# Another way to turn float64 weights into float32, a planner's order, and additions moved to VectorE

## The chip, the cores and the metric

The kernel runs on one core of a Trainium2 chip. The metric is the device time of one launch in microseconds (us). Three runs of the kernel before gave 1403.98, 1405.87 and 1405.85 us; the median is 1405.85.

## The reference

Three blocks follow one another, for a batch of 4, 448 tokens and 768 channels:

```
attention:  scores = q k^T / 8;  30 * tanh(scores / 30);  softmax;  times v        (12 heads of 64)
mixer:      u = x + (relu(x^T w_tok1) w_tok2)^T;   x = u + relu(u w_ch1) w_ch2     (768 -> 1536 -> 768)
FNet:       u = x + real(fft(fft(x, tokens), channels));  un = (u - mean) / std(u)
            out = u + relu(un w_ch1) w_ch2                                         (768 -> 3072 -> 768)
```

All weights of the two mixer blocks come as float64 (the generator scales float32 by a float64 number), so the kernel gets 64-bit words and has to make float32 of them.

## The kernel before, in words

**Precision.** Each float32 operand of the large products is split into a high part in the fast format (fp32r) and a low part, the difference. A product is three matmuls: high with high (L248), high weight with low data (L249), low weight with high data (L250); the helper is `mm3`. Each is 448 columns wide.

**Stages.** Attention runs first, in 24 pairs of heads. Then comes the first pair of channel products (`c1`, `c2`): 6 groups of 2 x 128 hidden channels, the first 3 in `group`, the others as visits. Between them and the last pair the Fourier step runs (`fold`, `transform`), spread over the visits. The second pair (`m1`, `m2`) has 12 groups for one half of the batch, again as visits, and then 6 Strassen groups (`up_steps`, `down_steps`) for the other half and for the combined blocks. `fold_in`, `fold_out`, `last15`, `last67` and `last23` add up the result tiles `z` at the end, and `store` writes them.

**A visit** has six steps. In each step `down` makes one tile of the output in PSUM (12 matmuls) and adds it into `z`. Between the steps the weights of the next visit are asked for, and at steps 2 and 3 the upper product of the next visit runs (`up`, 36 matmuls each), followed by `hidden`, which makes the relu and the split. A weight tile holds both halves of the 128 x 768 weights, and there are four such slots (`w`): two lower weights of this visit, two upper ones of the next.

**Weights.** `piece` makes a weight tile from a float64 block: `convert`, then `halves` (a ScalarE copy for the high part, a subtraction for the low one on VectorE or GpSimd). `convert` loads the block so that a byte lands ahead of each word, and then works in two strands. ScalarE makes a power of two from the top byte in three `Relu` steps (clamped from below, from above, and turned round), VectorE shifts the low word and sets an exponent (L359), adds the two powers as 16-bit words, and multiplies mantissa and power (L368). `convert_v`, for the token weights and the first two `c1` blocks, does it with VectorE steps alone but one (L313 to L323). In the second pair most pieces are also written to DRAM (`put`, `keep`) and fetched again for the Strassen groups (`fetch`, `fetch_x`); `combine` makes the Strassen sums of four pieces with subtractions on VectorE or GpSimd. Sixteen pieces are made ahead (`ahead`), during the first three groups of the first pair.

**The order.** The program's order on every engine comes from `Plan.run`, which is run when the program is built. Every operation has costs by engine (`v(n)` for VectorE, `vp(n)` for VectorE or GpSimd, whichever ends first in the plan, `a(n)` for ScalarE), worked out from the width n and from a fixed part in `fixed`. The planner keeps the operations sorted by their place in the code plus a shift by key (`SHIFT`), looks at the first few hundred, and takes the one that can start first; of those within 0.1 us, the one that stands first. `fixed` holds 0.065, 0.05 and 0.16 us (VectorE, ScalarE, GpSimd) while attention is described, and is set to 0.15, 0.14 and 0.3 before the rest is. Two `c1` blocks and the first splits (`split_u`) belong to the rest but are placed among attention.

Of the kernel before, what the change touches and what calls it, by code (L numbers as in the profile page):

```python
# [34 lines left out]
G = 2  # L35
RCOL = 904
TW = 8 * NE
MIN_NORMAL = 1.125 * 2.0 ** -15
SK1, SK2 = 3, 2
# [16 lines left out]
class Op:  # L56
# [9 lines left out]
    "den": -2446, "den<": -1603, "den>": -713, "exp": -90, "gather": -60, "late": 0, "wx": -40, "piece": -40, "exp<": -590, "exp>": -922, "load": 61,  # L66
# [143 lines left out]
def kernel(  # L210
# [58 lines left out]
    def t(n):  # L269
        return {"T": n / 2210}  # L270
# [60 lines left out]
    def convert(src, rows, cols, x=None):  # L331
# [12 lines left out]
        def cat(i):  # L344
            return cv()[i][:rows, :cols]

        def power(out, src, scale, bias, reads, writes):
            copy(cols, out, src, reads, writes, AF.Relu, scale=scale, bias=float(bias))
# [16 lines left out]
        def value():  # L365
            return (x() if x else raw().rearrange("p a b -> p (a b)").bitcast(F32))[:rows, :cols]
# [25 lines left out]
    def piece(src, x=None, k=None, dve=False):  # L392
        w, ws = w_slot()
        if dve:
            convert_v(src, 128, DM, part(w, 0), part(w, 1), ws[1:], [w])
        else:
            value, key = convert(src, 128, DM, x)
            halves(DM, value, part(w, 0), part(w, 1), [key, w], ws[1:])
            if k is not None:
                put(value, [key], k)  # L400
        return w, ws
# [333 lines left out]
    def phase_ce():  # L735
# [18 lines left out]
        def cut(q, w, f, kc):  # L754
            ws, wr = w[kc // NJ if q else f]
            c = f * NS + kc % NJ * 128 if q else kc * 128
            return ws, wr, slice(c, c + 128)
# [15 lines left out]

        def hidden(ps, y=None, fine=False):
            rh, rl = r_slot(F32R), r_slot(F32R)
            for bs in ((0,), (1,)) if fine else ((0, 1),):
                b0, n = bs[0], len(bs)
                kp, kh, kl = ([(x, b) for b in bs] for x in (ps, rh, rl))

                def at(x, b0=b0, n=n):  # L780
                    return pair(x)[:, b0:b0 + n, :]

                def src(b0=b0, n=n):
                    return ps()[:, b0:b0 + n, :S]

                if y is None:
                    copy(n * S, lambda at=at: at(rh), src, kp + [ps, rh], kh, AF.Relu)
                    pl.op(v(n * S), lambda e, at=at, src=src: V.scalar_tensor_tensor(
                        out=at(rl), in0=src(), scalar=0.0, in1=at(rh), op0=ALU.max, op1=ALU.subtract
                    ), kp + kh + [ps, rh, rl], kl)  # L790
                else:
                    pl.op(v(n * S), lambda e, at=at, src=src: V.scalar_tensor_tensor(
                        out=src(), in0=src(), scalar=0.0, in1=at(y), op0=ALU.max, op1=ALU.mult
                    ), [y, ps], kp)
                    copy(n * S, lambda at=at: at(rh), src, kp + [ps, rh], kh)
                    tt(v(n * S), lambda at=at: at(rl), src, lambda at=at: at(rh), ALU.subtract,
                       kp + kh + [ps, rh, rl], kl)
            return rh, rl

        def down(q, ws, r, bp, kc, y=None, apart=False):  # L800
            ps = mm_slot()
            zz = z[bp][kc]


            def mm(b, ps=ps):
                for fs in [[f] for f in range(G)] if apart else [list(range(G))]:
                    reads = [ps]
                    for f in fs:
                        reads += cut(q, ws, f, kc)[1] + list(r[f, bp]) + [(x, b) for x in r[f, bp]]

                    def mms(e, fs=fs):
                        for f in fs:
                            rh, rl = r[f, bp]
                            w, _, s = cut(q, ws, f, kc)
                            mm3(ps()[:, b, :S], w()[0][:, s], w()[1][:, s],
                                pair(rh)[:, b, :], pair(rl)[:, b, :], f == 0, f == G - 1)

                    pl.op(t(3 * len(fs) * S), mms, reads, [(ps, b)])

            def add(b0, n, ps=ps):  # L820
                tt(v(n * S), lambda: zz[:, b0:b0 + n, :], lambda: ps()[:, b0:b0 + n, :S], lambda: zz[:, b0:b0 + n, :],
                   ALU.add, [ps] + [(ps, b) for b in range(b0, b0 + n)], zk(bp, kc)[b0:b0 + n])

            mm(0)
            mm(1)
            if y is not None:
                pl.op(v(W2), lambda e: V.tensor_tensor(out=both(ps), in0=both(ps), in1=pair(y), op=ALU.mult),
                      [y, ps], [(ps, b) for b in range(2)])
            add(0, 2)

# [330 lines left out]
        wu = [piece(c1[f], dve=True) for f in range(G)]  # L1161
        split_u(0)
        split_u(1)

# [5 lines left out]
        def group(w1, w2, g, wu, u, nxt, between):  # L1170
# [15 lines left out]
            for bp in range(NB2):  # L1186
                for i, kc in enumerate(KORD):
                    down(0, wd, r, bp, kc)
# [66 lines left out]
        UPS, UPS2 = (2, 3), (2, 3)  # L1255
# [20 lines left out]
        AHEAD = [(n % 2, n // 2, n < 4 * SK2) for n in range(16)]  # L1276
# [12 lines left out]
        seq = [(0, g, bp) for bp in range(NB2) for g in range(NB, NGC)]  # L1289
        seq += [(1, g, 0) for g in range(NGM)]  # L1290
        kept = {}

        sh = [[None] * (NGM // 2) for _ in range(2)]
        held = {}

        def combine(q, g):
            x11, x21, x12, x22 = xs = [held.pop((q, 4 * g + i), None) or u_slot(F32) for i in ((0, 1, 2, 3) if q else (0, 2, 1, 3))]
            for x, i in ((1, 2), (3, 3), (0, 0), (2, 1)) if not q else ((1, 1), (3, 3), (0, 0), (2, 2)):
                if xs[x].first is None:
                    get(lambda x=x: xs[x]()[:, :DM], [], [xs[x]], fh[q][4 * g + i])  # L1300
# [11 lines left out]
        JOBS = {(4, 2): (0, 0), (5, 2): (1, 0), (6, 2): (0, 1), (7, 2): (1, 1)}  # L1312

        def weights(q, g, f, n):
            if q:
                k = G * g + f
                if (n, k) in early:
                    return fetch(early[n, k])
# [532 lines left out]
```

## Time and profile before

| | |
|---|---|
| median of three runs | 1405.85 us |
| profiled execution | 1406.29 us, its span 1404.4 us |
| TensorE matmul busy | 1365.7 us, 97% |
| VectorE busy | 1073.5 us, 76% |
| ScalarE busy | 704.1 us, 50% |
| GpSimd busy | 321.5 us, 23% |
| mean granted TensorE clock | 0.994 |

The span runs from the first to the last instruction. PE is TensorE, DVE is VectorE, ACT is ScalarE, POOL is GpSimd, SP is SyncE, which issues the DMAs. Nearly all elementwise operations are recorded by helpers, so L279 is any operation of two tensors and L276 any ScalarE step; the tile names tell them apart (`z<-mm,z` adds a PSUM tile into the output, `r<-mm,r` is the low half of a hidden tile). Matmuls overlap, so their durations add up to more than the time that passes. A row of the windows view gives a stretch (from:to in us), its length, the busy time and the number of instructions of PE, PEld (its weight loads), DVE, ACT and POOL, then the granted TensorE clock as a share of full speed, the DMA engines' busy share and GB/s. In other rows an arrow `<-` behind a number names what ended the idle time or the wait.

### The profile page before, as it was taken

How to read it: one execution, taken by the hardware profiler on the slowest of the kernel's cores; microseconds unless marked ns; L12 is line 12 of the kernel's file. 1: busy time of each engine (PE TensorE's matmuls, PEld its weight loads, DVE VectorE, ACT ScalarE, POOL GpSimd, SP SyncE). 2: the span in 40 equal slices, each digit the busy share in tenths (PEclk: the TensorE clock that was granted, in tenths of full speed). 3: DMA queues.
4: the chain of work that ended last, by engine and by line, in shares of the span. 5: the costliest groups of instructions: out<-in, count | busy, mean ns of one | idle time of the engine just before them, and what ended most of it. 6: DMA issues, size and time to landing. Idle time of an engine off the chain costs nothing.

```text
span 1404.4 us, 18761 instructions
## 1 busy us (share of the span) xinstructions
PE 1365.7 (97%) x7470; PEld 1135.0 (81%) x7470; DVE 1073.5 (76%) x1153; ACT 704.1 (50%) x824; POOL 321.5 (23%) x169
## 2 busy tenths in 40 slices
PE   8899999999999999999998999999999999999996
PEld 3344444599999999899998989988989998999996
DVE  7999988566776756557889699888977646667688
ACT  7878887576555544123233235444544553543432
POOL 4342433100000001000001122432314404414354
PEclk9999999999999999999999999999999999999999
DMA  4223221015666566512231168787868433344452
GB/s 125 86 73 105 83 73 47 7 68 157 247 201 194 193 222 207 160 46 91 90 136 57 46 223 298 272 309 259 301 229 298 152 113 100 103 124 133 130 178 99
DMA packets 67353, 211.90 MB, mean 151 GB/s; under 512 B 7552, under 2 KB 8960, under 8 KB 67266
## 3 DMA queue, kind: packets, MB, share of 16 engines
q1 hardware_dynamic: 66112, 208.08, 44.4%
q0 software_dynamic: 1152, 2.62, 0.7%
q8 instruction: 59, 0.97, 0.3%
q14 instruction: 28, 0.23, 0.0%
q10 hardware_dynamic: 2, 0.00, 0.0%
HBM read 145.30 MB, written 65.37 MB: 150 GB/s over the span
## 4 chain that ended last, share of the span: by engine, by line
PE 70%; DVE 15%; ACT 6%; DMA 5%; issue 2%; POOL 1%; SPq 0%; DVEq 0%; ACTq 0%; POOLq 0%
PE mm L249 20%; PE mm L248 20%; PE mm L250 20%; DVE t L279 3%; PE av L579 3%; DVE m L279 2%; DMA raw<-in_m_dram 2%; DMA wl<-kept 2%; PE sc L511 2%; DVE z L279 2%; ACT t L536 2%; ACT t L516 2%; PE av L595 2%; DVE u L279 2%; PE mx L706 1%
## 5 line engine op out<-in xcount | busy, mean ns | idle before, releaser
L249 PE MATMUL mm<-u,wh 128*128 128x448 f32 x798 | 293.7, 368 | 0.2 <-DVE u L279 0.2
L248 PE MATMUL mm<-u,wh 128*128 128x448 f32 x774 | 284.9, 368 | 4.9 <-DVE z L279 3.3
L250 PE MATMUL mm<-u,wl 128*128 128x448 f32 x774 | 284.6, 368 | 2.3 <-DMA wl<-kept 2.3
L279 DVE TENSOR_TENSOR z<-mm,z 128x896 f32<-128x896 f32 (+1 forms) x210 | 214.0, 1031 | 62.8 <-PE mm L250 61.4
L248 PE MATMUL mm<-r,wh 128*128 128x448 f32 x696 | 255.7, 367 | 0.7 <-DVE r L279 0.3
L249 PE MATMUL mm<-r,wh 128*128 128x448 f32 x678 | 249.4, 368 | 6.9 <-DVE r L279 6.6
L250 PE MATMUL mm<-r,wl 128*128 128x448 f32 x696 | 254.9, 366 | 0.0
L249 PEld LDWEIGHTS mm<-u,wh 128*128 128x128 f32 x798 | 151.1, 189 | 13.0 <-DVE u L279 0.6
L248 PEld LDWEIGHTS mm<-u,wh 128*128 128x128 f32 x774 | 146.5, 189 | 18.1 <-issue 3.7
L250 PEld LDWEIGHTS mm<-u,wl 128*128 128x128 f32 x774 | 146.5, 189 | 15.3 <-DMA wl<-kept 2.7
L276 ACT ACTIVATE cva<-raw 128x768 bf16<-128x768 int8 x70 | 63.4, 906 | 172.0 <-DVE u L368 66.4
L249 PEld LDWEIGHTS mm<-r,wh 128*128 128x128 f32 x678 | 127.8, 188 | 19.7 <-DVE r L279 8.7
L248 PEld LDWEIGHTS mm<-r,wh 128*128 128x128 f32 x696 | 131.2, 188 | 13.0 <-ACT r L276 0.8
L250 PEld LDWEIGHTS mm<-r,wl 128*128 128x128 f32 x696 | 131.2, 188 | 10.9
L528 POOL PARTITION_ALL_REDUCE mb<-m x48 | 93.6, 1997 | 166.9 <-DVE m L279 151.0
L276 ACT ACTIVATE r<-mm 128x896 fp32r<-128x896 f32 (+5 forms) x81 | 66.6, 826 | 119.2 <-PE mm L250 54.6
L279 DVE TENSOR_TENSOR t<-t,mb 112x1792 f32<-112x1792 f32 x48 | 107.3, 2254 | 5.5 <-POOL mb L528 5.4
L516 ACT ACTIVATE t<-sc,scl 112x896 f32<-112x896 f32 x96 | 92.4, 1004 | 12.4 <-PE sc L511 6.4
L276 ACT ACTIVATE wh<-wl 128x768 fp32r<-128x768 f32 x57 | 48.1, 845 | 95.3 <-DMA wl<-kept 93.8
L511 PE MATMUL sc<-qr 64*112 64x448 f32 x384 | 88.1, 569 | 7.7 <-ACT t L516 7.7
L536 ACT ACTIVATE t<-t,cap_sb 112x1792 f32<-112x1792 f32 x48 | 85.3, 1789 | 14.4 <-DVE t L279 14.1
L579 PE MATMUL av<-t,v 112*32 112x448 f32 x768 | 78.2, 542 | 2.0 <-ACT t L536 1.6
(205 smaller groups left out, 2238.1 us busy)
## 6 DMA issues: line engine op xcount, KB each, us to landing
raw<-in_m_dram SPq DMA_DIRECT2D x48, 767.6 KB, 5.1
wl<-kept SPq DMA_DIRECT2D x86, 384.0 KB, 3.5
kept<-u SPq DMA_DIRECT2D x60, 384.0 KB, 5.3
raw<-in_c_dram SPq DMA_DIRECT2D x22, 767.6 KB, 5.1
kept<-y SPq DMA_DIRECT2D x32, 384.0 KB, 5.7
wh<-kept SPq DMA_DIRECT2D x29, 384.0 KB, 3.1
raw<-kept SPq DMA_DIRECT2D x29, 384.0 KB, 3.1
qr<-in_qk_dram SPq DMA_DIRECT2D x23, 448.0 KB, 3.3
```

The costliest lines, as they stand in the source:

```text
L248: T.matmul(out=dst, lhsT=wh, rhs=xh, start=first, stop=False, skip_group_check=more)
L249: T.matmul(out=dst, lhsT=wh, rhs=xl, start=False, stop=False, skip_group_check=more)
L250: T.matmul(out=dst, lhsT=wl, rhs=xh, start=False, stop=last, skip_group_check=more)
L276: pl.op(a(n), lambda e: A.activation(out=out(), in_=src(), func=func, **kw), reads, writes)
L279: pl.op(engs, lambda e: eng[e].tensor_tensor(out=out(), in0=in0(), in1=in1(), op=op), reads, writes)
L511: T.matmul(out=ps()[:CP, k, :S], lhsT=qr()[d, S + c * CP:S + (c + 1) * CP], rhs=qr()[d, :S], start=True, stop=True)
L516: pl.op(a(W2, 0.06), lambda e, c=c, ps=ps: A.activation(out=tl()[:, c], in_=ps()[:CP, :, :S], func=AF.Tanh, scale=scl[:CP, 0:1]), [ps, tl] ...
L528: pl.op({"P": 1.9}, lambda e, k=k: P.partition_all_reduce(mb()[:, k], mx()[:, k], CP, bass_isa.ReduceOp.max), [mx, mb], [kb], hold=0.75)
L536: pl.op(a(2 * W2, 0.1), lambda e, k=k: A.activation(out=tl()[:, :, k], in_=tl()[:, :, k], func=AF.Exp, scale=cap_sb[:CP, 0:1]), [tl], [ke])
L579: T.matmul(out=ps()[d, :S], lhsT=vv()[:, c, d], rhs=tl()[:, c, hd], start=(c == 0), stop=(c == NCH - 1))
L595: T.matmul(out=ps()[32 * k:32 * k + 32, :S], lhsT=ones[:CP, 0:32].bitcast(F32), rhs=tl()[:, c, hd], start=(c == 0), stop=(c == NCH - 1))
L706: T.matmul(out=ps()[:, :S], lhsT=channels_of(rt()[:, tb, c], kc % NJ), rhs=wt[:, tb, :], start=False, stop=last, skip_group_check=True)
```

## The change

`convert` gets other steps. The top byte goes through one `Relu` and two `Prelu` steps on ScalarE: the first clamps it from below, the second bends it at the other end (the negative side is scaled by 2^-40, the positive one kept), the third turns it into the exponent field of a float32 as an integer. VectorE then makes one `scalar_tensor_tensor`: the low word shifted right by 5, or'ed with that field. The shift L359 and the 16-bit addition go.

```diff
-        power(lambda: cat(0), top, 2048.0, (7 - 16 * 56) * 128, [raw], [cv, ca])
-        power(lambda: cat(1), top, -2048.0, 32768 - (7 + 16 * 72) * 128, [raw, cv], [cf])
-        power(lambda: cat(1), lambda: cat(1), -1.0, 32768, [cv], [cf])
-        pl.op({"V": 0.07 + cols / 1920}, lambda e: V.tensor_scalar(
-            out=word(), in0=word(), scalar1=5, scalar2=112 << 23,
-            op0=ALU.logical_shift_right, op1=ALU.bitwise_or,
-        ), [], [raw])
-        tt({"V": 0.07 + cols / 1920}, lambda: cat(0).bitcast(U16), lambda: cat(0), lambda: cat(1), ALU.add,
-           [cv, cf], [ca])
...
+        copy(cols, step, top, [raw], [cv, ca], AF.Relu, bias=72.0)
+        copy(cols, step, step, [cv], [ca], AF.Prelu, scale=-1.0, bias=16.0, alpha=KINK)
+        copy(cols, field, step, [cv, ca], [cf], AF.Prelu, scale=-FIELD / KINK, bias=-112.0 * FIELD, alpha=KINK)
         pl.op(v(cols), lambda e: V.scalar_tensor_tensor(
-            out=value(), in0=word().bitcast(F32), scalar=-256.0, in1=cat(0), op0=ALU.mult, op1=ALU.mult,
-        ), [raw, cv, ca], [x or raw])
+            out=value(I32), in0=word(), scalar=5, in1=field(), op0=ALU.logical_shift_right, op1=ALU.bitwise_or,
+        ), [raw, cv, cf], [x or raw])
```

The step lengths of the planner change later than before: `fixed.update` moves behind the two `c1` blocks and the first splits. The additions of the Strassen groups into `z` (`gather`) lose their shift of -60 places; the additions of the visits get the same key, with a shift of 0.

```diff
-    "den": ..., "gather": -60, "late": 0, ...
+    "den": ..., "gather": 0, "hid": 0, "late": 0, ...
...
         wu = [piece(c1[f], engs=v) for f in range(G)]
         split_u(0)
         split_u(1)
+        fixed.update(V=0.15, A=0.14, P=0.3)
...
-        fixed.update(V=0.15, A=0.14, P=0.3)
         phase_ce()
```

All additions of `z` tiles to one another at the end may only run on VectorE, and the last tile is added in two halves:

```diff
-            tt(vp(S), lambda: a[:, 1, :], lambda: a[:, 1, :], lambda: a[:, 0, :], ALU.add, ka[:1], ka[1:])
+            tt(v(S), lambda: a[:, 1, :], lambda: a[:, 1, :], lambda: a[:, 0, :], ALU.add, ka[:1], ka[1:])
             for x, k in ((zl, kc), (zh, NJ + kc)):
-                tt(vp(W2), lambda x=x: x, lambda x=x: x, lambda: a, ALU.add, ka, zk(1, k))
+                tt(v(W2), lambda x=x: x, lambda x=x: x, lambda: a, ALU.add, ka, zk(1, k))
... (the same in fold_out, last15 and last67)
         def last23(kc, ps):
-            gather(1, kc, 0, 2, ps, 0, False)
-            store(1, kc, kc == NJ - 1)
+            end = kc == NJ - 1
+            for b in range(2) if end else (0,):
+                gather(1, kc, b, 1 if end else 2, ps, b, False)
+            store(1, kc, end)
```

The visits are rewritten as two classes, `First` and `Half`, with the same matmuls. One order changes: the second lower weight of a visit of the second pair is asked for ahead of step 1, behind the upper weights of the next visit; before, it was asked for after step 0, ahead of them. The pieces made ahead come in another order (`AHEAD`: four of `m1`, four of `m2`, and so on, instead of one of each in turn), and as many of them as before.

```diff
-                if q and i == 0 and len(x[4]) < 2:
-                    x[4].append(weights(q, g, 1, 1))
-                if i == (0 if q else 1) and not ending:
-                    a_, b_, c_ = seq[n + 1]
-                    nxt = visit(a_, b_, c_, [weights(a_, b_, f, 0) for f in range(G)])
...
+                if i == 1:
+                    x.below(1)
+                x.down(i, kc)
...
+                if i == int(one):
+                    nxt.above()
+                if i in UPS:
+                    if i == UPS[0]:
+                        nxt.below(0)
+                    nxt.up(UPS.index(i))
```

## Rows read from the trace of the kernel before

**Rows 1.** Windows by stage; the columns stand in the section on the profile above.
```profile
0.00:290.00 290.00, 276.01 (x2001) 134.17 (x2002) 246.00 (x235) 219.68 (x236) 94.28 (x54) 1.00 0.24 72
290.00:830.00 540.00, 532.48 (x2760) 491.52 (x2760) 392.21 (x489) 221.76 (x275) 35.24 (x23) 0.99 0.44 146
830.00:1060.00 230.00, 225.47 (x1093) 205.85 (x1092) 201.66 (x217) 117.86 (x145) 63.45 (x33) 0.99 0.78 276
1060.00:1355.00 295.00, 293.26 (x1439) 269.71 (x1439) 192.99 (x179) 131.08 (x153) 104.42 (x49) 1.00 0.46 146
1355.00:1404.40 49.40, 38.44 (x184) 33.71 (x182) 40.68 (x37) 13.72 (x19) 24.11 (x10) 0.97 0.32 112
sum 1404.40, PE 1365.66 PEld 1134.96 DVE 1073.54 ACT 704.10 POOL 321.49; mean PE 273.13 PEld 226.99 DVE 214.71 ACT 140.82 POOL 64.30
```

**Rows 2.** Waits of TensorE, whole run: us in total, times, longest.
```profile
PE sc L511 <- ACT t L516: 7.7, 16, 1.7
PE mm L249 <- DVE r L279: 6.6, 6, 1.8
PE mm L248 <- DVE z L279: 6.4, 3, 3.3
PE mm L250 <- DMA wl<-kept: 2.3, 1, 2.3
```

**Rows 3.** The same windows view, right after a long wait.
```profile
767.40:773.00 5.60, 5.56 (x15) 4.98 (x16) 5.60 (x6) 1.66 (x2) 0.00 (x0) 0.51 0.00 0
```

**Rows 4.** Groups by form, whole run: name, count, busy us, mean ns, idle before.
```profile
L276 ACT ACTIVATE cva<-raw 128x768 bf16<-128x768 int8 x70 | 63.4, 906 | 172.0 <-DVE u L368 66.4 <-DMA raw<-in_m_dram 33.8 <-DMA raw<-in_c_dram 32.3
```

**Rows 5.** Groups by form on VectorE, 830 to 1060 us.
```profile
L368 DVE SCALAR_TENSOR_TENSOR u<-raw,cva 128x768 f32<-128x768 f32 x31 | 34.3, 1105 | 1.2
L279 DVE TENSOR_TENSOR cva<-cva,cvf 128x768 uint16<-128x768 bf16 x31 | 22.0, 710 | 7.4 <-ACT cvf L276 7.2
L359 DVE TENSOR_SCALAR raw<-raw 128x768 int32<-128x768 int32 x31 | 21.7, 701 | 2.5 <-DMA raw<-in_m_dram 2.5
```

**Rows 6.** Timeline of VectorE, 150 to 166 us: start, us, engine, line, operation.
```profile
159.52 0.98 DVE L317 SCALAR_TENSOR_TENSOR cva<-raw,cva 128x768 int32<-128x768 int32 x1
160.54 1.57 DVE L320 SCALAR_TENSOR_TENSOR cva<-raw,cva 128x768 int32<-128x768 int32 x1
```

**Rows 7.** Waits of TensorE, 830 to 1060 us.
```profile
PE mm L249 <- DVE r L279: 4.3, 4, 1.8
```

**Rows 8.** Timeline before the wait that ends at 1037.82 us.
```profile
1033.33 1.97 DVE L279 TENSOR_TENSOR wl<-u,wh 128x768 fp32r<-128x768 f32 x1 [1.78 <-ACT wh L276]
...
1035.22 0.54 DVE L279 TENSOR_TENSOR cva<-cva,cvf 128x768 uint16<-128x768 bf16 x1
...
1037.82 0.47 PE L249 MATMUL mm<-r,wh 128*128 128x448 f32 x1 [1.84 <-DVE r L279]
```

**Rows 9.** Group of ScalarE's table loads, whole run.
```profile
L1710 ACT ACT_TABLE_LOAD x1 | 1.3, 1283 | 1.3 <-PEq L1836 1.3
```

**Rows 10.** Groups by form behind 1355 us.
```profile
L279 POOL TENSOR_TENSOR z<-z 128x896 f32<-128x896 f32 x6 | 15.8, 2642 | 4.8 <-DVE z L279 4.8
L279 DVE TENSOR_TENSOR z<-z 128x896 f32<-128x896 f32 x6 | 10.2, 1722 | 0.0
...
L279 DVE TENSOR_TENSOR z<-mm,z 128x896 f32<-128x896 f32 x3 | 3.2, 1084 | 0.7 <-PE mm L250 0.7
```

**Rows 11.** Timeline of the end (seven stores are merged in one row).
```profile
1383.95 0.47 PE L249 MATMUL mm<-r,wh 128*128 128x448 f32 x1 [1.64 <-DVE r L279]
...
1394.45 6.20 SPq L1167 DMA_DIRECT2D out_dram<-z  x7
...
1395.48 0.47 PE L248 MATMUL mm<-y,wh 128*128 128x448 f32 x1 [2.89 <-DVE z L279]
...
1398.22 1.62 DVE L279 TENSOR_TENSOR z<-mm,z 128x896 f32<-128x896 f32 x2 [0.74 <-PE mm L250]
```

**Rows 12.** Windows view of the stretch before the last freed tile.
```profile
1376.10:1394.30 18.20, 14.84 (x72) 12.95 (x70) 18.10 (x14) 3.32 (x5) 12.32 (x5) 1.00 0.00 1
```

More of the change, by code (lines that the diff above doesn't have):

```diff
@@ L342, in top, with step, field, value @@
             return raw().bitcast(I8)[:rows, :cols, 4]
[L344 to L348, printed above, removed]
+        def step():
+            return cv()[0][:rows, :cols]
+        def field():
+            return cv()[1].bitcast(I32)[:rows, :cols]
+        def value(dt=F32):
+            return (x().bitcast(dt) if x else raw().rearrange("p a b -> p (a b)").bitcast(dt))[:rows, :cols]
         pl.op(
@@ L771, in up, with hidden @@
             return ps
-        def hidden(ps, y=None, fine=False):
+        def hidden(ps, y=None):
+            pl.key = "hid"
             rh, rl = r_slot(F32R), r_slot(F32R)
[L776 to L797, printed above, removed]
@@ L1275, in phase_ce @@
         HL = 8
-        AHEAD = [(n % 2, n // 2, n < 4 * SK2) for n in range(16)]
+        AHEAD = [(q, 4 * g + i, not g) for g in range(2) for q, i in
+                 ((0, 0), (0, 1), (0, 2), (0, 3), (1, 0), (1, 2), (1, 1), (1, 3))]
         def between_c(g):
@@ L1288, in phase_ce @@
         ys = [None, None]
[L1289 to L1290 removed]
         kept = {}
[L1293 removed]
+        NG = NGM // 2
+        sh = [[None] * NG for _ in range(2)]
         held = {}
         def combine(q, g):
[L1297 to L1300, printed above, removed]
+            ix = (0, 1, 2, 3) if q else (0, 2, 1, 3)
+            x11, x21, x12, x22 = xs = [held.pop((q, 4 * g + i), None) or u_slot(F32) for i in ix]
+            for n in (1, 3, 0, 2):
+                if xs[n].first is None:
+                    get(lambda n=n: xs[n]()[:, :DM], [], [xs[n]], fh[q][4 * g + ix[n]])
             sh[q][g] = ks = [home() for _ in range(4)]
@@ L1341, in weights, with __init__, above, below @@
             return w, ws
-        def ups(x, f):
-            q, g, bp, w, wd, r = x
-            if not q or f == 0:
-                wd.append(weights(q, g, f, 1))
-            r[f, bp] = hidden(up(q, w, f, bp, (u, un)[q]), ys[bp] if q and g else None)
-        def visit(q, g, bp, w):
-            return [q, g, bp, w, [], {}]
+        class First:
+            def __init__(self, g, bp):
+                self.g, self.bp, self.wd, self.r, self.order = g, bp, [], {}, KORD
+            def above(self):
+                self.w = [first(self.g, f, 0) for f in range(G)]
+            def below(self, half):
+                pass
+            def up(self, f):
+                self.wd.append(first(self.g, f, 1))
+                self.r[f, self.bp] = hidden(up(0, self.w, f, self.bp, u))
+            def down(self, i, kc):
+                fs = [(f, cut(0, self.wd, f, kc)) for f in range(G)]
+                down([[x] for x in fs] if i < 2 else [fs], self.r, self.bp, kc)
+        class Half:
+            def __init__(self, v):
+                self.v, self.r, self.order, self.wd = v, {}, range(NK), [None] * 2
+            def above(self):
+                self.w = [second(0, 2 * self.v + i) for i in range(2)]
+            def below(self, half):
+                if self.wd[half] is None:
+                    self.wd[half] = second(1, 2 * self.v + half)
+            def up(self, f):
+                self.r[f, 0] = hidden(up(1, self.w, f, 0, un), ys[0] if self.v else None)
+            def down(self, i, kc):
+                fs = [(f, cut(1, self.wd, f, kc)) for f in range(G)]
+                down([[x] for x in fs] if i < 2 else [fs], self.r, 0, kc, None if self.v else ys[0])
         def enter(bp, i, kc):
@@ L1354, in enter @@
             if bp and i == 1:
-                x = visit(*seq[0], [weights(0, NB, f, 0) for f in range(G)])
-                entered.append(x)
+                seq[0].above()
             if bp and i in UPS1:
-                ups(entered[0], UPS1.index(i))
+                seq[0].up(UPS1.index(i))
         def homes_of(q, g):
@@ L1655, in phase_ce @@
                     pl.groups = ("second",)
-                if nxt:
-                    for f in range(G):
-                        if i == (UPS2 if q != nxt[0] or q and bp != nxt[2] else UPS)[f]:
-                            ups(nxt, f)
-            if not q and g == NGC - 1:
-                steps, at = transform(mx[bp]), 0
-            x = nxt
+                    continue
+                for x_ in JOBS.get((n, i), ()):
+                    combine(*x_)
+                if i == int(one):
[4 more added lines that the diff above has]
+                    nxt.up(UPS.index(i))
+            if turn_:
+                steps, at = transform(mx[x.bp]), 0
         pl.groups = ()
```

160 lines of the change are left out of this document (85 added, 75 removed).

## The prediction

> **What bounds the kernel now.** I read the profile from the coarse view to the fine one. The windows by stage [rows 1] come first: TensorE is busy for 1365.66 of 1404.40 us, VectorE for 1073.54, ScalarE for 704.10, GpSimd for 321.49. From 290 us on the matmuls come back to back: in 1060 to 1355 us, 1439 of them in 293.26 us, 0.204 us each. What can be won there is the time in which TensorE waits. The waits of TensorE over the whole run [rows 2] name who ends them: VectorE with 6.6 us (it wrote a low half r) and with 6.4 us (it added into z and so freed a PSUM tile), one DMA with 2.3 us. The 7.7 us of the score matmuls belong to attention. A long wait also costs afterwards: after the 3.3 us wait that ended at 767.4 us, the granted clock was 0.51 for 5.6 us, the 1.2 GHz level, and 15 matmuls took that time, 0.373 us each [rows 3]; against 0.204 us that is another 2.5 us. So this kernel is bound by TensorE, and the change can win or lose what VectorE's lateness costs, some 15 us behind attention, the end of the program, and whatever the order in attention does.
>
> **The conversion of the weights.** It runs 70 times: each time ScalarE works three times in a row, 906 ns for the first [rows 4], and VectorE runs a shift (L359), a 16-bit addition (line 279 into cva) and a product (L368). The change keeps three ScalarE instructions with the same 768 elements. The last now writes 32-bit words; for each I keep the length of the first, so ScalarE's part counts as nothing. On VectorE the shift and the addition go, and the product becomes one shift-and-or on the same two inputs. The place where this counts is 830 to 1060 us, where 31 conversions run and VectorE is busy for 201.66 of 230 us [rows 1]. There the shift took 701 ns and the addition 710 ns on average, the product 1105 ns [rows 5]. So 31 x 1.411 = 43.7 us leave VectorE in that stage, and its share falls from 88% to 69%. What replaces the product is not in the trace as such. Its nearest row is the shift-and-or on 768 int32 words of the other conversion, 0.98 us [rows 6]; the same kind a moment later beside a GpSimd reduction took 1.57 us [rows 6]. I take 1.1 us, no change, as the product's mean already holds such collisions; at 1.57 us each the stage would get 31 x 0.47 = 14.6 us back of the 43.7.
>
> What of that reaches TensorE? It waits 4.3 us in four places there, each time for a low half r from VectorE [rows 7]. The worst is the 1.84 us wait that ends at 1037.82 us; in front of that low half VectorE's queue holds the 16-bit addition of a conversion (1035.22, 0.54 us), its product, and before them the subtraction of another weight, which took 1.97 us [rows 8]. With the addition gone the low half is at least 0.54 us earlier. More is possible, as the 701 and 710 ns above are means over collisions with GpSimd. The low bound is four waits x 0.6 = 2.4 us; the high one is all 4.3 plus about 1.5 us of half clock (the mean clock of the stage is 0.99 [rows 1], so up to 2.3 us were lost to it). I take 3.5 us. The other 39 (by the code 38 belong to the first pair and to the pieces made ahead) run mostly before 690 us, where the clock and VectorE leave room; I count them as nothing, hidden behind the matmuls (this cover holds as long as VectorE is below about 90%, and it is at 392.21 of 540 us [rows 1]).
>
> A page of the Trainium skill speaks against the Prelu steps: "ScalarE: Activation LUTs", section on table sets, names tanh, relu and abs beside exp for the set that attention needs, leaves the rest of its 15 functions open, and does not name Prelu; it says that a function outside the active set costs a load. The trace has one load in the whole program, 1283 ns [rows 9]; no run here shows whether Prelu brings more. That result is a rival below.
>
> **The last additions on VectorE.** Behind 1355 us GpSimd makes six additions of whole z tiles (896 wide) at 2642 ns each; VectorE makes six more at 1722 ns; those that read PSUM take 1084 ns for the same width [rows 10]. I read the difference as the two engines slowing one another where both read SBUF; the six on VectorE lose 6 x (1722 - 1084) = 3.8 us by it. TensorE waits here twice: 1.64 us until 1383.95 for a low half r that stands behind such additions, and 2.89 us until 1395.48 for a PSUM tile that an addition frees [rows 11]. The change puts all of them on VectorE and takes the collisions away. From 1376.1 us to the addition that frees the tile at 1394.3 VectorE has no room left: 14 operations, 18.1 of 18.2 us [rows 12]. Seven of these are a whole tile wide, six half, one a weight; undisturbed they would take 7 x 1.08 + 6 x 0.6 + 0.9 = 12.1 us (0.6 for half the width is an estimate from 1.08). GpSimd's five operations there, four whole additions and a half one, are 4.9 us on VectorE: together 17.0. So at worst, with all of them ahead of the addition that frees the tile, 1.1 us are won; at best both waits go, 1.6 + 2.9 = 4.5 us. I take 3.
>
> **The end.** The last matmul ends at 1398.2 us. Then VectorE adds a whole tile and a half one, 1.62 us together, and SyncE issues the last of seven stores by 1400.65 [rows 11]; the program ends at 1404.4. With the last tile added in two halves, only a 0.6 us half follows the last matmul: at least 1.08 - 0.6 = 0.5 us; if the other half addition also moves ahead of the last matmul, and the last stores stand less closely behind one another (some 0.4 us each), 1.0 + 0.9 = 1.9 us at most. I take 1.
>
> **What is only moved.** The second lower weight of a visit is asked for after the two upper ones of the next visit, not before them. It is used later than these (its fourth step against the third), so the order is that of use; its slot comes free at the end of the visit before, three steps of 12 x 0.204 = 2.4 us and six times six matmuls (7.3 us) before it is needed, 14.6 us. I count 0, with the bounds -2 and +5 (two weights that come 2.5 us late, as the one of the DMA in [rows 2]). The step lengths that the planner uses for two conversions and the first splits change the order in attention: 290 us, in which VectorE is busy for 246.00 us [rows 1] and score matmuls wait 7.7 us [rows 2]. The trace shows no other order; I take 0 and as bounds 4 us either way, half of those waits. The additions of the Strassen groups lose 60 places of priority: TensorE is idle for 1.7 us in 1060 to 1355 us, so there is little to win (-1) and something to lose (the third rival).
>
> **The sum** against the profiled execution (1406.29 us, span 1404.4, 1.9 us around it): -3.5 (weights) -3 (last additions) -1 (end) = -7.5, so 1398.8 us. The median of the runs is 0.4 us below the profiled one; I forecast 1398 us.
>
> **Rivals.**
> - *The whole of VectorE's lateness goes.* The planner, with 0.94 us less for each conversion, also spreads the rest better: 5.8 in the middle, 4.5 and 1.9 at the end, and the 3.3 + 2.5 us at 767 us, where VectorE stands in collisions too: -18, 1388 us. For it: VectorE ends 13.0 us of waits in [rows 2], the DMA 2.3. Against: 767 us has no conversion.
> - *The relief is hidden.* TensorE's waits in 830 to 1060 us stay, because the low half waits for ScalarE, which runs the same three steps; the fresh collisions eat the rest. Only the end is left: -1 to -2, 1404 us, no change that can be told. Against: in [rows 8] VectorE's own queue stands in front.
> - *Additions without priority (slower).* In the six Strassen groups the additions that free PSUM tiles fall behind the low halves of the step before, which are ready earlier. Four tiles cover 4 x 2.4 = 9.8 us of TensorE; the rival decides from nine low halves in a row, 9 x 1.08. Then each group waits some 2 us and pays 1.4 us of half clock: 6 x 3.4 = 20, less 7.5: 1418 us. If half of the groups do it, 1409. For it: 60 places; against: today's slack, 293.26 of 295 us busy.
> - *Attention gets worse by 4 us* and the two weights come late (5 us): 1398 + 9 = 1407, up to 1410 with a half clock behind each wait.
> - *Table loads.* If Prelu needs another set than the steps between conversions, each conversion brings two loads: 70 x 2 x 1.28 = 180 us on ScalarE; in 830 to 1060 us 80 us on top of 117.86 [rows 1]. It fits, barely, and makes each weight 2.6 us later: with a wait of that size at every second one, 35 x 2.6 = 91 us, about 1490.
>
> **Chances.** Forecast (1392 to 1402.9): 0.57. All lateness goes (below 1392): 0.15. Hidden: 0.12, of which 0.10 counts as no change. Additions without priority 0.08, attention 0.06, of which 0.02 stays within the bound; table loads 0.02. 0.2% of the median is 2.8 us, about what a measurement of this kernel can tell from no change; so faster (below 1403.0) 0.74, same 0.12, slower (above 1408.7) 0.14. The range 1386 to 1409 leaves out the tails of the first rival and most of the third.
>
> **What would show it.** In the profile after: no 16-bit addition into cva and no L359-like shift, the shift-and-or near 1.0 us, VectorE's share in the stage of the weights near 70%, fewer low-half waits there; behind 1355 us no GpSimd z addition, VectorE's at 1.08 us, no wait of TensorE above 1 us; a half addition after the last matmul. I am wrong if waits for z appear in the Strassen stage, if attention ends more than 4 us from 290 us, if a second table load appears, or if the shift-and-or takes 1.5 us.

## The result, and the profile after

The changed kernel takes 1389.55 us (median; 1386.41 to 1391.81), against 1405.54 us for the kernel before in the same comparison: a ratio of 0.9887, 95% interval 0.9864 to 0.9910, or some 16 us less. The forecast was 1398 us, 7.5 us less. The direction and the range held; the size was half of what was measured. The profiled execution, 1386.41 us with a span of 1384.6 us, is the shortest of the four runs, so its stages add up to more (19.8 us) than the medians do.

Both profiles hold 7470 matmuls, so the place of the gain can be found by counting: the matmul with a given number starts some time earlier in the changed kernel, and this lead grows by 3.2 us in attention, by 2.9 us from 290 to 690 us, by 5.3 us from there to 830 us (the wait at 767 us), by 6.1 us in 830 to 1060 us and by 2.5 us from there to 1342 us (times of the kernel before). Behind that it does not grow: from the matmul that starts at 1342 us to the end of the span the kernel before takes 62.4 us, and the changed one 62.6 us.

The windows by stage, with the columns of [rows 1]; the last window ends with the span:

```profile
0.00:290.00 290.00, 278.20 (x2019) 137.64 (x2020) 247.39 (x238) 222.99 (x240) 93.95 (x54) 1.00 0.24 75
290.00:830.00 540.00, 535.99 (x2791) 494.17 (x2789) 355.32 (x415) 228.60 (x282) 34.00 (x23) 1.00 0.46 151
830.00:1060.00 230.00, 229.85 (x1128) 211.94 (x1129) 169.53 (x157) 116.42 (x141) 79.20 (x40) 1.00 0.78 284
1060.00:1355.00 295.00, 292.17 (x1428) 268.78 (x1427) 198.88 (x199) 132.20 (x155) 60.66 (x31) 0.99 0.43 136
1355.00:1384.60 29.60, 22.97 (x108) 19.96 (x108) 22.01 (x27) 5.32 (x8) 4.51 (x2) 0.93 0.28 107
sum 1384.60, PE 1359.18 PEld 1132.48 DVE 993.12 ACT 705.52 POOL 272.31; mean PE 271.84 PEld 226.50 DVE 198.62 ACT 141.10 POOL 54.46
```

VectorE works 80 us less (1073.54 before), ScalarE as long as before. In the stage of the weights VectorE is busy for 169.53 of 230 us, 74%, and TensorE stands still for 0.15 us, not 4.5. The first window holds 18 matmuls more than before: attention is ahead by some 3 us. The waits of TensorE, the whole run, as in [rows 2]:

```profile
PE sc L507 <- ACT t L512: 6.7, 13, 1.8
PE mm L251 <- DVE r L281: 2.4, 2, 1.8
...
PE mm L252 <- DMA wl<-kept: 1.5, 1, 1.5
...
PE mm L250 <- DVE z L281: 0.9, 2, 0.6
```

The low halves went from 6.6 to 2.4 us, the additions into z from 6.4 to 0.9. The groups of the new conversion on ScalarE over the whole run, and the table load (compare [rows 4] and [rows 9]); then VectorE's in 830 to 1060 us (compare [rows 5]):

```profile
L278 ACT ACTIVATE cva<-raw 128x768 bf16<-128x768 int8 x70 | 62.8, 898 | 122.5 <-DMA raw<-in_m_dram 86.0 <-DMA raw<-in_c_dram 36.4
...
L278 ACT ACTIVATE cvf<-cva 128x768 int32<-128x768 bf16 x70 | 59.1, 844 | 4.6 <-DVE y L364 2.9
L278 ACT ACTIVATE cva<-cva 128x768 bf16<-128x768 bf16 x70 | 58.9, 841 | 1.7
...
L1725 ACT ACT_TABLE_LOAD x1 | 1.3, 1283 | 1.3 <-PEq L1850 1.3
```

```profile
L364 DVE SCALAR_TENSOR_TENSOR u<-raw,cvf 128x768 int32<-128x768 int32 x29 | 34.3, 1184 | 23.7 <-ACT cvf L278 23.7
```

The three ScalarE steps cost what they cost before (898, 841 and 844 ns; 906, 891 and 845 ns before). There is still one table load in the program, and the 140 Prelu steps brought no other. The Trainium skill's page "ScalarE: Activation LUTs", in its section on table sets, names tanh, relu and abs beside exp and leaves the rest of the set open; the trace shows that the set loaded here holds Prelu. The shift-and-or takes 1184 ns where the product took 1105. ScalarE's first step also no longer waits for VectorE (66.4 us in [rows 4]); it waits for the DMA of the weights. And the end, the additions of z tiles behind 1335 us, as in [rows 10]:

```profile
L281 DVE TENSOR_TENSOR z<-z 128x896 f32<-128x896 f32 x12 | 14.4, 1218 | 0.0
```

All twelve are on VectorE, at 1218 ns instead of 1722 and 2642. Both waits of [rows 11] are gone. In their place TensorE waits 1.76 us for a low half at 1348.64 us, with a half clock behind it, and 1.07 us at 1355.0 us for a z tile that ScalarE copies, and the end as a whole is not shorter.

### The profile page after: what moved, and what is told of

It reads as the page before. It is cut to its first block, busy times and chain, and to the rows that moved or that the text cites. A ratio compares the mean times of both kernels' runs of the same rounds, so it can differ in the third digit from the quotient of the medians.

```text
span 1384.6 us, 18652 instructions
## 1 busy us (share of the span) xinstructions
PE 1359.2 (98%) x7470; PEld 1132.5 (82%) x7470; DVE 993.1 (72%) x1033; ACT 705.5 (51%) x824; POOL 272.3 (20%) x150
## 4 chain that ended last, share of the span: by engine, by line
PE 83%; DVE 10%; ACT 4%; DMA 1%; issue 1%; DVEq 0%; ACTq 0%
PE mm L250 23%; PE mm L252 23%; PE mm L251 23%; PE av L575 3%; PE sc L507 3%; DVE t L281 3%; DVE z L281 2%; DVE m L281 2%; PE mx L702 2%; PE av L591 2%; ACT t L532 1%; ACT t L512 1%; DVE u L281 1%; DMA wl<-kept 1%; DVE r L281 1%; PE av L602 1%
## 5 line engine op out<-in xcount | busy, mean ns | idle before, releaser
L252 PE MATMUL mm<-u,wl 128*128 128x448 f32 x786 | 287.8, 366 | 1.9 <-DMA wl<-kept 1.5
L278 ACT ACTIVATE r<-mm 128x896 fp32r<-128x896 f32 (+5 forms) x87 | 71.9, 831 | 114.9 <-PE mm L252 60.1
L281 POOL TENSOR_TENSOR wl<-wl,wh 128x768 fp32r<-128x768 f32 x17 | 32.3, 1900 | 333.2 <-DMA wl<-kept 196.7
```

Of the source, the lines that this page charges most:

```text
L252: T.matmul(out=dst, lhsT=wl, rhs=xh, start=False, stop=last, skip_group_check=more)
L278: pl.op(a(n), lambda e: A.activation(out=out(), in_=src(), func=func, **kw), reads, writes)
L281: pl.op(engs, lambda e: eng[e].tensor_tensor(out=out(), in0=in0(), in1=in1(), op=op), reads, writes)
```

## The experiments

Each ratio is to the kernel before, from runs on the same chip, with its 95% interval. The changed kernel stands at 0.9887; 0.001 is 1.4 us. "Alone" is one part in the kernel before, "undone" the changed kernel without it.

| part | alone | undone | worth when undone |
|---|---|---|---|
| conversion | 0.9949 [0.9936, 0.9962] | 0.9933 [0.9916, 0.9950] | 6.5 us |
| step lengths | 0.9962 [0.9950, 0.9974] | 0.9903 [0.9888, 0.9918] | 2.2 us |
| last additions | 0.9988 [0.9978, 0.9999] | 0.9925 [0.9906, 0.9943] | 5.3 us |
| order of the weights | 0.9952 [0.9939, 0.9966] | 0.9905 [0.9890, 0.9921] | 2.5 us |
| Strassen priority | 1.0014 [1.0003, 1.0025] | 0.9881 [0.9866, 0.9895] | -0.8 us |

(For the last additions, undone leaves the last tile in two halves.) The last column is the difference to 0.9887 times 1405.5 us. It adds up to 15.7 us, beside 15.9 measured; the parts alone add up to 19. The interval of the changed kernel is already 3.2 us either way, and a difference of two ratios carries some 4 us, so in the last column only the conversion and the last additions are clear of zero, and the close sum is luck. For the other parts the column "alone" and the places in the traces decide.

**The conversion, alone.** `convert` of the changed kernel in the kernel before; work and planned order both change.

> Only convert is changed: new steps, and with them the planner's order. The changed kernel is 19.8 us shorter in the profiled execution: 3.1 in attention, 2.3 at the DMA wait of 571 us, some 5 at the wait of 767 us, 7.5 in 830 to 1095 us, 2.3 in the first Strassen groups, nothing at the end. Theory 'conversion': the 7.5 and most of the 5 at 767 are there (the planner moves everything behind the first conversion), attention is not: -9 to -13 us, 1393 to 1396. Rival 'the rest of the change': the order of the weights and the step lengths made the gain; then 0 to -4, above 1401.

1399.62 us, ratio 0.9949: 7.2 us. It is less than expected because the stall at 767 us stayed (3.8 us here). In 830 to 1060 us the matmuls gain 5.8 us, of the 7.5 expected up to 1095.

**Its work without its order.** The two VectorE steps stay in the plan and emit nothing:

```diff
-        pl.op({"V": 0.07 + cols / 1920}, lambda e: V.tensor_scalar(
-            out=word(), in0=word(), scalar1=5, scalar2=112 << 23, ...), [], [raw])
-        tt({"V": 0.07 + cols / 1920}, lambda: cat(0).bitcast(U16), ..., ALU.add, [cv, cf], [ca])
+        pl.op({"V": 0.07 + cols / 1920}, lambda e: None, [], [raw])
+        pl.op({"V": 0.07 + cols / 1920}, lambda e: None, [cv, cf], [ca])
```

> The order of before to the last instruction, with the new conversion's work: the two VectorE steps that go are still planned, but issue nothing. Theory 'work' (VectorE's time is what counts): the waits for low halves in 830 to 1060 us shrink from 4.3 to below 1.5 us and the half clock behind 1037 us goes, -4 to -6 us; the 767 us wait stays. Rival 'order' (the gain comes from how the planner lays out the rest when conversions are shorter): below -2 us here.

1398.38 us, ratio 0.9947 [0.9934, 0.9960]: the same gain with the old order. In the stage of the weights TensorE never waits (window, columns as above):

```profile
830.00:1060.00 230.00, 230.00 (x1131) 212.11 (x1131) 163.48 (x160) 121.60 (x148) 68.30 (x35) 1.00 0.79 284
```

All 4.3 us of [rows 7] are gone, and with them the half clock behind 1037 us; VectorE fell to 163.48 us. The gain is what the conversion itself does, not a better plan: first of all VectorE's time. (That ScalarE no longer waits for VectorE comes with it and was not tried apart.)

**The order with the old work.** The changed kernel, with two more VectorE steps issued ahead of each shift-and-or. Their results are used nowhere, and the planner does not know of them:

```diff
+            V.tensor_tensor(out=step().bitcast(U16), in0=step(), in1=step(), op=ALU.add)
+            V.tensor_scalar(out=cv()[0].bitcast(I32)[:rows, :cols], in0=word(), scalar1=5, scalar2=112 << 23,
+                            op0=ALU.logical_shift_right, op1=ALU.bitwise_or)
```

> The changed kernel's order to the last instruction, but each conversion carries two more VectorE steps in front of the shift-and-or, a 16-bit addition and an int32 shift of the old shapes, whose results nobody uses. Theory 'work': the weights' stage gives back what the conversion brought, 4 to 8 us, about 1395. Rival 'order': the new order would do without the saved time, under 2 us.

1415.13 us, ratio 1.0067 [1.0053, 1.0082], 25 us above the changed kernel: three times the upper expectation. Its groups in 830 to 1060 us, then its waits there:

```profile
L371 DVE TENSOR_SCALAR cva<-raw 128x768 int32<-128x768 int32 x31 | 23.5, 758 | 1.1
L370 DVE TENSOR_TENSOR cva<-cva 128x768 uint16<-128x768 bf16 x31 | 21.6, 697 | 22.2 <-ACT cvf L278 22.2
```

```profile
PE mm L250 <- DVE z L281: 3.9, 2, 2.2
PE mm L251 <- DVE r L281: 3.3, 5, 1.0
PE mm L250 <- ACT wh L278: 1.6, 1, 1.6
```

The steps are as long as the old ones, so it is the same load on VectorE. It also loses 11 us before 495 us, where the prediction counted conversions as hidden. Both steps stand behind the last ScalarE step here, where the old shift could run earlier, and they tie ScalarE to VectorE again (in 830 to 1060 us its first step waits 53.9 us for L371), so this is not the old conversion to the letter; the next run is.

**The old conversion, planned, in the changed kernel.** `convert` of the kernel before.

> The changed kernel with the old conversion, its two VectorE steps planned as they were. Putting the same two steps in unplanned cost 25 us. Theory 'planned work costs what it took away': +6 to +9 us, 1396 to 1399, in 830 to 1095 us. Rival 'the new order cannot carry the work, planned or not': +15 us or more, above 1404.

1395.53 us, 6.5 us more, as the first theory has it. Planned, the old steps cost 6.5 us, and the unplanned ones cost 25; how much of that difference is the missing plan and how much their place behind the last ScalarE step is not shown.

**The step lengths, alone.** Only `fixed.update` moves.

> Only the place of the step lengths (0.065, 0.05, 0.16 us kept for two conversions and the first splits). Theory 'attention order': the first matmul of the channel products starts at about 290 us instead of 293.0, and the time falls by 2 to 4 us. Rival 'nothing': under 1 us, and the 3.1 us of the changed kernel come from another part. The other stages may move either way with the new order.

1401.30 us, 5.3 us less by the ratio. Its first window shows the attention of the changed kernel, 2019 matmuls by 290 us against 2001 in [rows 1]:

```profile
0.00:290.00 290.00, 278.19 (x2019) 137.61 (x2020) 247.35 (x238) 223.00 (x240) 92.47 (x54) 1.00 0.25 75
```

The channel products start at 289.9 us, not 293.0. The other 2 us arise in 830 to 1060 us, and in the next run they are not found.

**The step lengths, undone.**

> The changed kernel with the step lengths set back ahead of the two conversions and the first splits. The prediction counted this part as 0 with 4 us either way; alone it brought 4.8 us, of which only 3.2 stood in attention. Theory 'attention alone': the first matmul of the channel products comes 3 us later and nothing else follows, +2 to +4 us against the changed kernel, 1392 to 1394. Rival 'the order behind it hangs on it too': +5 us or more.

1391.56 us, +2.2 us, at the lower end of the first theory but within the uncertainty. The channel products start at 293.6 us again, and the 2.9 us that the changed kernel gains from 290 to 690 us are gone too; the run with the old conversion planned lacks them as well. So they need both parts.

**The last additions, alone.**

> Only the last additions on VectorE and the last tile in two halves. The prediction gave -4 us for this. After the result I expect 0 to -2: in the changed kernel the stretch behind 1342 us is not shorter than before, VectorE's queue holds the additions one after another. Rival (the prediction's own): both waits of before, 1.64 and 2.89 us, go and the end is 1 us shorter, -4 us or more.

1404.21 us, 1.7 us less, as expected. TensorE ends its last matmul at 1391.1 us, 7.1 us earlier, but VectorE its last addition only 3.6 us earlier. Its last rows (start, us):

```profile
1394.53 1.08 DVE L279 TENSOR_TENSOR z<-z 128x896 f32<-128x896 f32 x1
...
1395.65 0.62 DVE L279 TENSOR_TENSOR z<-mm,z 128x448 f32<-128x448 f32 x1
```

It still adds for 5 us after the last matmul, and the span ends 9.0 us after it (6.3 us before). The wait for a tile became a queue behind TensorE. The runs on the priority below show whose doing that is.

**The last additions, undone**: `vp` for `v` in the four functions.

> The changed kernel with the last additions open to GpSimd again (the last tile still in two halves). Theory 'given back': on VectorE the additions stand in front of a low half at 1348 us and cost what they win at the end, so 0 to +2 us. Rival (the prediction's mechanism): two waits of TensorE at the end return, +3 us or more.

1394.88 us, +5.3 us: my theory falls, and two waits return. The additions of this kernel on GpSimd behind 1335 us, and its waits there:

```profile
L281 POOL TENSOR_TENSOR z<-z 128x896 f32<-128x896 f32 x4 | 10.1, 2558 | 0.1
```

```profile
PE mm L251 <- DVE r L281: 3.6, 1, 3.6
PE mm L250 <- DVE z L281: 2.5, 1, 2.5
```

The wait for a z tile is that of [rows 11]. The one for a low half is not: it ends at 1352.3 us, 39 us before the end and not 20, where the changed kernel waits too, for half as long. That the engines slow one another is seen in front of it. GpSimd makes three of its additions of z in 1340.66 to 1348.67 us and a subtraction behind them, and two operations of VectorE's queue take 2.91 and 2.68 us (timeline of this kernel) that take 1.09 us each in the changed one:

```profile
1346.71 2.91 DVE L1506 SCALAR_TENSOR_TENSOR y<-y,r 128x896 f32<-128x896 f32 x1
...
1349.54 2.68 DVE L281 TENSOR_TENSOR r<-r,u 128x896 fp32r<-128x896 f32 x1
```

In the changed kernel, ahead of its low half at 1348.64 us, VectorE's queue holds two of the moved additions and an operation held up by GpSimd (timeline):

```profile
1339.19 1.08 DVE L281 TENSOR_TENSOR z<-z 128x896 f32<-128x896 f32 x1
1339.73 2.25 POOL L281 TENSOR_TENSOR raw<-raw 128x768 fp32r<-128x768 f32 x1 [2.00 <-ACT raw L278]
1340.19 2.73 DVE L281 TENSOR_TENSOR r<-r 128x896 fp32r<-128x896 f32 x1
...
1342.85 1.08 DVE L281 TENSOR_TENSOR z<-z 128x896 f32<-128x896 f32 x1
...
1348.64 0.47 PE L251 MATMUL mm<-r,wh 128*128 128x448 f32 x1 [1.76 <-DVE r L281]
```

**The order of the weights, alone** (with that of the pieces made ahead, which was not tried by itself; up to 690 us TensorE is 0.4 us ahead):

```diff
+                if q and i == 1 and len(x[4]) < 2:
+                    x[4].append(weights(q, g, 1, 1))
                 down(q, x[4], ...)
...
-                if q and i == 0 and len(x[4]) < 2:
-                    x[4].append(weights(q, g, 1, 1))
```

> The kernel before with two moves alone: the second lower weight of a visit is asked for ahead of step 1, behind the upper weights of the next visit, and the pieces made ahead come in the new order. Theory 'weights in the order of use': the stall at 767 us (3.3 us and 2.5 us of half clock), which conversion, step lengths and last additions left in place, goes, and perhaps the DMA wait at 571 us; -3 to -6 us. Rival 'nothing moves' (the prediction counted these moves as 0): under 1.5 us either way.

1399.36 us, 6.7 us less by the ratio. The 3.3 us wait at 767 us is gone, with one of 1.6 us at 758.6 us in its place; the DMA wait at 571 us (2.4 us) is not. From 690 to 830 us the matmuls gain 4.6 us. The prediction had 0.

**The order of the weights, undone.**

> The changed kernel with the second lower weight asked for after step 0 again, ahead of the upper ones, and the old order of the pieces made ahead. Theory 'weights in the order of use': the stall at the Fourier step (767 us before) comes back, +4 to +7 us, 1394 to 1397. Rival: with the lighter conversion the order no longer matters, under 2 us.

1391.79 us, +2.5 us: between the two theories, and within the uncertainty. The stall returns with 3.74 us, and its cause can be read (timeline of this kernel, then the subtractions of the same two upper weights in the changed kernel):

```profile
757.12 2.86 DVE L281 TENSOR_TENSOR wl<-wl,wh 128x768 fp32r<-128x768 f32 x1
...
759.90 1.68 DVE L281 TENSOR_TENSOR z<-r,z 128x446 f32<-128x446 f32 x3
761.51 4.07 DVE L281 TENSOR_TENSOR z<-mm,z 128x896 f32<-128x896 f32 x4
...
762.73 0.71 PE L250 MATMUL mm<-u,wh 128*128 128x448 f32 x1 [3.74 <-DVE z L281]
```

```profile
746.23 1.85 POOL L281 TENSOR_TENSOR wl<-wl,wh 128x768 fp32r<-128x768 f32 x1 [188.64 <-DMA wl<-kept]
...
748.50 0.96 DVE L281 TENSOR_TENSOR wl<-wl,wh 128x768 fp32r<-128x768 f32 x1 [1.24 <-ACT wh L278]
```

In the old order the lower weight is fetched first and the second upper weight only at 751.51 us; its subtraction stands on VectorE ahead of the additions that free PSUM tiles, and takes 2.86 us beside GpSimd. In the new order both upper weights are asked for by 742.59 us. GpSimd takes the subtraction of the first, and that of the second is done on VectorE 8.6 us sooner, in 0.96 us and ahead of the crowded stretch. From 690 to 830 us the changed kernel gains 5.3 us, this one 0.3. The profiled executions differ by 5.4 us in the end and the medians by 2.2 us, as that of the changed kernel is the shortest of its runs.

**The priority of the additions.** Three runs: `"gather": -60` in the changed kernel (which moves the visits' additions too, as they carry the key now); a key of its own with -60 for the Strassen additions alone; and `"gather": 0` in the kernel before.

> The changed kernel with the additions of the Strassen groups 60 places ahead again, and with them those of the visits that now carry the same key. The prediction held 0 for the loss of the places (-1 to +20). Theory: 0 to +3 us (in the run with only the last additions changed the program ended 9.0 us after the last matmul, against 6.2 in both others; with 60 places the end should look like that again). Rival: -2 us, the places would still be worth having.

1402.06 us, ratio 0.9970 [0.9960, 0.9981], 11.7 us more than the changed kernel and outside both theories.

> The changed kernel with the 60 places of priority back for the Strassen additions alone; the additions of the visits stay at 0, as in both kernels. The run that moved both keys was 12 us longer than the changed kernel, and 7 of these arose at the Fourier step, before any Strassen group. Theory 'the visits' key did that': 0 to +4 us against the changed kernel, 1390 to 1394, all of it behind 1060 us. Rival 'the Strassen priority itself': above 1398.

1388.67 us, no difference to the changed kernel in the time.

> The kernel before with the shift of the Strassen additions at 0 and nothing else. With GpSimd open for the last additions the changed kernel lost 4.7 us behind 1342 us. Theory 'the two belong together': the same loss here, the end 3 to 5 us later, little before it: 1406 to 1411, no gain. Rival 'the priority was a brake': -2 us or more, in 1060 to 1340 us.

1407.64 us, 2 us more. Behind 1342 us it loses 5.8 us against the kernel before, as the first theory has it, and up to there it was 5.1 us ahead. Of these 5.1 us, 2.2 are the 1.59 us wait at 1179.5 us of the kernel before and what follows it, which this run does not have; for the rest I have no reason from this run alone. So the Strassen priority is worth little in the whole time, and the loss of the first run is the visits' key.

At the end, though, the priority and the last additions belong together. The time from the matmul that starts at 1342 us in the kernel before to the end of the span, in us:

| | last additions open to GpSimd | on VectorE alone |
|---|---|---|
| 60 places | 62.4 (the kernel before) | 62.0 (last additions alone), 61.6 (Strassen 60) |
| no priority | 68.1 (this run), 67.1 (last additions undone) | 62.6 (the changed kernel) |

These are single executions; the other runs lie at 62.0 to 63.6 (top left), 62.7 (top right) and 61.1 to 63.0 (bottom right). So only the field at the bottom left stands out. The additions on VectorE are worth some 5 us where the priority is gone, and what they bring where it is kept is within that spread; the change took both, and at the end the two cancel. The queue behind TensorE goes with the priority: with VectorE alone and 60 places the span ends 8.6 to 9.0 us after the last matmul in all three kernels, and 5.9 us after it in the changed one.

Back to the first run, with the visits' additions moved too: TensorE waits at the Fourier step, never more than 0.9 us at a time, and the clock falls to the 1.2 GHz level for some 6.8 us (that kernel's window):

```profile
715.00:735.00 20.00, 16.55 (x74) 13.82 (x75) 11.84 (x20) 8.69 (x12) 0.00 (x0) 0.83 0.21 79
```

**No GpSimd at all behind attention's reductions**: `vp` returns VectorE only.

> The changed kernel with no elementwise operation on GpSimd at all: what the planner could give to either goes to VectorE. GpSimd's additions hold up VectorE where both read SBUF, but they also carry work. Theory 'VectorE's time is the bound': VectorE gets some 85 us more (178 us of GpSimd at half its rate, plus overhead, less the collisions), in 830 to 1060 us its share goes back to about 85% and the waits for low halves return: +3 to +8 us, 1393 to 1398. Rival 'collisions are what hurts': without them the time falls, 1382 to 1387.

1391.38 us, ratio 0.9902 [0.9888, 0.9916]: 2 us more, inside the uncertainty of the changed kernel's ratio. Neither theory: VectorE got 37 us more, not 85 (sum row), the low halves waited 0.3 us in all. What kept the balance are durations (groups in 830 to 1060 us):

```profile
sum 1389.00, PE 1361.92 PEld 1134.46 DVE 1030.02 ACT 706.78 POOL 96.72; mean PE 272.38 PEld 226.89 DVE 206.00 ACT 141.36 POOL 19.34
```

```profile
L281 DVE TENSOR_TENSOR u<-u 128x768 f32<-128x768 f32 x47 | 44.9, 955 | 1.0
L281 DVE TENSOR_TENSOR wl<-u,wh 128x768 fp32r<-128x768 f32 x30 | 28.0, 951 | 5.6 <-ACT wh L278 5.6
L364 DVE SCALAR_TENSOR_TENSOR u<-raw,cvf 128x768 int32<-128x768 int32 x29 | 27.6, 952 | 12.9 <-ACT cvf L278 11.8 <-PE mm L251 1.1
```

The shift-and-or takes 952 ns, 1184 in the changed kernel.

## Why the prediction found only half of the gain

**What bounds the kernel: right.** TensorE gained what VectorE's lateness had cost: the two kinds of waits of [rows 2] that VectorE ends fell from 13.0 to 3.3 us, and TensorE's busy time by 6.5 us for the same matmuls.

**The conversion: mechanism right, size halved.** The price of every step was close (1.1 us against 1184 ns, ScalarE unchanged, no load). The term "I take 3.5 us" is 6.5 to 7.4 us. In the stage of the weights the changed kernel gains 6.1 us, and 1.0 with the old conversion. I shortened each of four waits by the operation that stood directly in front of it and took a value nearer to the low bound of 2.4 than to the high one of 5.8. The run with the old order shows all four gone together with their half clock: a low half is late because the queue in front of it has not drained, and with 38 us less in the stage (201.66 to 163.48) it drains. The high bound was the better reading, and it left out what the other conversions are worth once the order is tight.

**Last additions and end: 4 us forecast, nothing found there.** The collisions are real (2.91 and 2.68 us for operations that take 1.09 without them), and both waits of [rows 11] went. But others came in their place, and the end is as long as before: 62.6 us against 62.4. The sum counted the lost places of priority apart from this, at 0 and for the Strassen groups alone; at the end they cost 5.8 us while GpSimd may still make the last additions, and moving these additions pays that back. So the 5.3 us when undone are no gain over the kernel before. In that kernel, with its priority kept, the move brings 1.7 us by the median. Between the last matmul and the end of the span the changed kernel takes 5.9 us, not 6.3; 1 us was forecast. The halved tile was not tried alone. That the total came out as near as half is partly luck: the sum had 4 us at a place that gave none.

**"What is only moved" counted as 0: this step failed, and it holds most of what is missing.** Alone in the kernel before, the step lengths are worth 5.3 us and the weights' order 6.7; undone 2.2 and 2.5, not clear of the uncertainty. In the traces the lead grows by 3.2 us in attention with the one and by 5.3 us from 690 to 830 us with the other, and neither growth is there without it. For the step lengths the bound of 4 us either way was there, without a reason for a sign. For the weights I had found that the new order is that of use, and still set the gain at 0, with a low bound of -2, because no wait of TensorE named a weight. The 767 us wait named an addition into z; the weight stood in VectorE's queue ahead of it. The first rival, whose numbers come nearest (1388 us), counted that wait but credited it to the planner's shorter conversions; the conversion alone left it.

**The rivals.** Additions without priority: refuted for the Strassen groups, where the changed kernel gains; the loss exists, but at the end and only with GpSimd in play. The relief is hidden: refuted by the stage's idle 0.15 us. Attention worse: it got 3 us better. Table loads: one, as before.

**What stays open.** Why the shorter planned steps give a better attention order is not shown; the planner's choices there were not followed one by one. Why the 2.9 us from 290 to 690 us need both the conversion and the step lengths, and why the wait at 1179.5 us goes in most of the runs, is open. The 2 us that the step lengths alone brought behind attention are within the spread of single executions.

## What to carry to other kernels

When one engine's queue feeds the bound engine, count what a change takes from the whole stage of that queue, not only the instruction in front of a wait; and read a wait's queue back to the last operation that did not belong there, as the operation named may only stand behind it. A move that follows the order of use is worth a number of its own when the queue that it feeds is nearly full, even if no wait names it. A part that is worth much when it is undone may only be paying for another part of the same change: set each stretch against the kernel before, too, and try the two parts in all four combinations.

## What the runs showed of the hardware

GpSimd's help was worth almost nothing here: taking its 176 us of elementwise work away (272.31 to 96.72 us) put only 37 us on VectorE. Operations with two SBUF inputs ran at 951 to 955 ns for 768 columns in 830 to 1060 us with GpSimd idle, and at 1060 to 1332 ns on average in the changed kernel, where GpSimd works for 79.20 of these 230 us. Prelu writing int32 from bf16 costs ScalarE 844 ns, as the step from bf16 to bf16 does (841 ns). A wait of TensorE as short as 1.76 us was followed by a stretch partly at the 1.2 GHz level (granted clock 0.66 over the next 4.4 us):

```profile
1348.60:1353.00 4.40, 4.36 (x15) 3.92 (x16) 4.40 (x5) 1.80 (x2) 0.00 (x0) 0.66 0.29 112
```
